# One kernel for sorted attention, a Fourier mix and an MLP: V of the first two batches mixed from its natural layout

## The chip, the cores and the metric

The kernel runs on one core of a Trainium2 chip. What counts is the device time of one execution, in microseconds (us). The engines named below are PE (TensorE: it loads a stationary operand and then streams a moving one past it), PEld (those loads of stationary operands, shown as a row of their own), DVE (VectorE), ACT (ScalarE), POOL (GpSimd, which here mainly starts transfers) and SP (SyncE, which starts the stores). "L945" is line 945 of the kernel; lines of the kernel before and of the changed kernel differ by up to some 16, and where both are meant the text says which.

## The reference

There are 4 batches, 8 heads, a sequence of 768 and 64 dimensions per head. `sort_net` holds an 8x8 matrix per batch and head. The rest in order, cut to what is computed:

```
P = sort_net
for _ in range(5):                       # on 8x8, per batch and head
    P = exp(P - max(P));  P = P / (rowsum + 1e-9);  P = P / (colsum + 1e-9)
k_sorted = einsum('bhij,bhjcd->bhicd', P, k in 8 blocks of 96 keys)
v_sorted = einsum('bhij,bhjcd->bhicd', P, v in 8 blocks of 96 keys)
attn     = softmax(0.125 * q_block @ k_sorted_block.T) @ v_sorted_block
x   = attn with heads side by side                     # 4 x 768 x 512
u   = x + real(fft(fft(x, axis=seq), axis=model))
un  = (u - mean(u)) / sqrt(var(u) + 1e-6)
out = u + maximum(un @ w_ch1, 0) @ w_ch2               # 512 -> 2048 -> 512
```

So 256 small matrices (4 batches x 8 heads x 8 blocks) mix the eight blocks of K and of V, attention runs inside a block of 96 keys, and the Fourier mix and the MLP then run over whole batches.

## The kernel before

**How the order of the work is set.** The program records every operation as an entry of a list, with a number. The table `ORDER` (written out as strings of numbers) gives for each of PE, DVE, ACT, POOL and SP the order in which that engine gets its entries. A scheduler then walks the tables and only picks PSUM banks and buffers. No engine leaves its order: an instruction whose input is late holds up everything behind it on its engine. Ahead of a point early in the program, PE waits are filled with dummy matmuls (L1973, "spins" below), which keep PE busy and have no reader.

**The start.** The 8x8 matrices are normalised on ACT and DVE (L766 to L776, tile `hr`), and spread into the block matrices `bdk` (for K, L805) and `bdv` (for V, L985) that serve as moving operands or stationary operands on PE.

**V of batches 0 and 1.** V is handled in two pairs of batches, t=0 (batches 0 and 1) and t=1 (batches 2 and 3). 128 partitions hold the (batch, head, block) triples of a pair; along a partition lie 96 keys of 64 dimensions. `v_path(t)` sums V over the keys (L873 on PE, L880 on DVE), which gives a mean that is handled apart. For t=0 the transfer puts V into the buffer `hr` (two transfers of 48 keys each), and eight copies (L903, issued through the helper at L855) rewrite it to `vcx` so that for one dimension d the 96 keys lie side by side; in that copy the keys of a block are also put in another order, (r, c) with r counting 6 and c counting 16. For t=1 a subtraction of the mean (L909) does the rewriting. `v_mix(t, e)` (L928) then does, for each of two halves e, 64 matmuls at L945: the stationary operand is 128 neighbouring columns of `vcx` starting at column 96d (96 columns for d=63), the moving operand 64 columns of `bdv`. Eight of them share a PSUM bank, and L951 adds the mean. The copy at L962 takes the bank to `vsf`/`vsb`, in front of the attention.

**K.** K is mixed by `bdk` on PE (L1140, L1170) and comes out of PSUM by a copy (L1148, L1178, again through L855; tile `ks`), with the keys in the same (r, c) order as V. Scores are L1236, the exponentials L1245, L1258 and L1260, the weighted sum of V L1275.

**The Fourier mix and the norm.** The work of a batch lies in two groups of three row tiles (T = 0 to 2 and T = 3 to 5). For a group of batch 0, the row sums of squares are taken on ACT (L1488), then one `Ln` (L1500) and one `Exp` (L1504) give the inverse of the deviation for the three row tiles, `nm` follows on DVE, `un` (L1518 on ACT, L1522 on DVE) is the normalised row, it is transposed, and the first MLP product L1558 reads it together with the weights `w1sb`. ACT evaluates `Exp` and `Ln` from tables which an instruction loads. At L711 the kernel asks for the set that has both functions, as the first thing on ACT.

**The MLP.** Batches 0 and 1 use plain products (L1558, L1615). Batches 2 and 3 use a scheme with seven products in place of eight (`ff1_seven`, L1694): some blocks of the hidden layer come out as a sum of a bank and a snapshot of another bank (`snap`, L1714 on ACT). DVE adds the two (L1702) and clamps the sum at zero (L1708). Second products are L1794, their sums L1811.

**The stores.** SP starts them in the order of its table. For T < 2 it is one transfer (L1583), or two halves (L1580); T = 2 takes three transfers (L1585, L1587, L1589); T > 2 goes through POOL (L1593).

Of the kernel before, what the change touches and what calls it, by code (L numbers as in the profile page):

```python
# [8 lines left out]

# [9 lines left out]
D = 64  # L19
NB = 8  # L20
# [46 lines left out]
    ),  # L67
    "ACT": (
# [24 lines left out]
    ),  # L93
    "DVE": (
# [1911 lines left out]
```

## Time and profile before

| what | value |
|---|---|
| median of 3 runs | 256.93 us (256.84 to 257.6) |
| span of the profiled execution | 254.8 us |
| PE busy | 245.2 us (96%), 2996 matmuls |
| DVE busy | 234.2 us (92%), 597 instructions |
| ACT busy | 165.3 us (65%), 376 instructions |
| POOL busy | 57.5 us (23%) |
| granted TensorE clock | full in all slices but the last |

Two things about reading it. The span runs from the first to the last recorded event of one profiled execution; the time that counts has about 2.1 us around it (256.93 - 254.8). And a matmul's record on PE is longer than the distance to the next one, since matmuls overlap: "busy" on PE means that something is in the pipe, not that PE could take nothing more. What PE needs per matmul is read from stretches in which many of the same kind follow each other, for instance in the chain of waits.

### The profile page before, as it was taken

To read this page: it belongs to the slowest core of one execution; us is meant where nothing else is said; L and a number is where in the kernel's file an instruction comes from. 1 tells how busy PE (TensorE), PEld (TensorE's weight loads), DVE (VectorE), ACT (ScalarE), POOL (GpSimd) and SP (SyncE) were. 2 spreads that over 40 slices of the span, in tenths; PEclk is the share of its full clock that TensorE was granted. 3 is DMA by queue.
4 is the path that set the end of the run, shared out by engine and by line. 5 is a ranking of instruction groups with operands and counts; after the bars stand their busy time and mean duration, and the time that the engine had idled before them with its cause. 6 is when DMAs were issued, how large, how long until landed. Compare 5 with 4: busy or idle time off the path is not lost.

```text
span 254.8 us, 7461 instructions
## 1 busy us (share of the span) xinstructions
PE 245.2 (96%) x2996; PEld 167.0 (66%) x2996; DVE 234.2 (92%) x597; ACT 165.3 (65%) x376; POOL 57.5 (23%) x88
## 2 busy tenths in 40 slices
PE   4999999999999999999999999999999999999992
PEld 1347875566566676644667757888657887567882
DVE  4799998999999989978999998999999999999993
ACT  2599998999968879956797377622687323773000
POOL 8974532234400770003100000210100000050013
PEclk9999999999999999999999999999999999999998
DMA  6999999999942699524132002530202400220025
GB/s 134 202 215 300 210 217 214 208 211 187 150 49 75 86 193 120 64 43 136 44 38 44 1 8 46 98 125 35 82 3 41 84 3 0 85 88 37 3 82 207
DMA packets 42809, 26.54 MB, mean 104 GB/s; under 512 B 30234, under 2 KB 39208, under 8 KB 42772
## 3 DMA queue, kind: packets, MB, share of 16 engines
q0 software_dynamic: 23664, 18.35, 42.9%
q1 hardware_dynamic: 19110, 7.71, 15.0%
q8 instruction: 23, 0.38, 0.6%
q14 instruction: 12, 0.10, 0.1%
HBM read 29.07 MB, written 6.29 MB: 139 GB/s over the span
## 4 chain that ended last, share of the span: by engine, by line
PE 71%; issue 9%; DVE 9%; ACT 8%; POOL 2%; DMA 1%; POOLq 0%; DVEq 0%
PE bank L1558 15%; PE bank L1794 14%; PE bank L1694 12%; PE bank L1615 9%; PE bank L1275 4%; PE bank L1440 3%; PE bank L945 2%; PE bank L1236 2%; ACT vcx L855 2%; PE bank L1349 2%; POOL out_dram L1593 2%; DVE rt L1292 1%; PE bank L1444 1%; PE bank L1047 1%; PE bank L1140 1%
## 5 line engine op out<-in xcount | busy, mean ns | idle before, releaser
L1558 PE MATMUL bank<-ut,w1sb 128*128 128x384 f16 x256 | 48.2, 326 | 0.0
L1714 ACT COPY vsf<-bank 128x384 f32<-128x384 f32 x48 | 21.6, 482 | 24.0 <-PE bank L1694 23.6
L1245 ACT ACTIVATE ex<-bank 96x384 f32<-96x384 f32 x64 | 29.3, 487 | 7.6 <-PE bank L1236 6.2
L1558 PEld LDWEIGHTS <-w1sb 128*128 128x128 f16 x256 | 23.1, 98 | 14.1 <-issue 0.3
L1570 ACT ACTIVATE hr<-bank 128x384 f16<-128x384 f32 x56 | 26.3, 491 | 8.5 <-PE bank L1558 8.5
L1593 POOL DMA_INDIRECT out_dram<-u,rows x9 | 9.4, 1042 | 97.4 <-DVE u L1811 72.5
L1794 PEld LDWEIGHTS <-hr 128*128 128x128 f16 x288 | 28.2, 98 | 4.6
L1702 DVE TENSOR_TENSOR hr<-bank,vsf 128x384 f16<-128x384 f32 x48 | 25.2, 548 | 1.6 <-PE bank L1694 1.0
L1615 PE MATMUL bank<-w2sb,hr 128*128 128x512 f16 x96 | 23.6, 380 | 0.0
L1794 PEld LDWEIGHTS <-vcx 128*128 128x128 f16 x216 | 21.1, 98 | 3.2
L1694 PE MATMUL bank<-ut,w1sb 128*128 128x384 f16 x96 | 20.7, 326 | 0.0
L1794 PE MATMUL bank<-w2sb,hr 128*128 128x256 f16 x144 | 18.7, 272 | 0.0
L1275 PEld LDWEIGHTS <-eb 97*128 97x128 f16 x416 | 15.7, 98 | 3.1 <-issue 0.4
L1794 PE MATMUL bank<-kq,vcx 128*128 128x256 f16 x144 | 17.5, 272 | 0.0
L1694 PEld LDWEIGHTS <-w1sb 128*128 128x128 f16 x128 | 12.5, 98 | 7.5
L612 POOL DMA_DIRECT2D kq<-in_q_dram x18 | 15.4, 866 | 8.8 <-PE bank L1558 4.2
L1292 DVE TENSOR_TENSOR rt<-bank,rz 128x384 f16<-128x384 f32 x32 | 16.9, 547 | 0.2
L1275 PE MATMUL bank<-vsf,eb 97*128 97x65 f16 x416 | 16.9, 193 | 0.0
L855 ACT CAST ks<-bank 128x384 f16<-128x384 f32 x27 | 14.4, 555 | 3.1 <-PE bank L1140 3.0
L1260 ACT ACTIVATE eb<-ex,negone 96x384 f16<-96x384 f32 x26 | 15.9, 616 | 0.1
L855 ACT CAST vsf<-bank 96x512 f16<-96x512 f32 x22 | 14.2, 679 | 1.4 <-PE bank L945 1.4
L1258 DVE TENSOR_SCALAR eb<-ex 96x384 f16<-96x384 f32 x38 | 13.9, 371 | 0.6 <-ACT ex L1245 0.4
(195 smaller groups left out, 535.5 us busy)
## 6 DMA issues: line engine op xcount, KB each, us to landing
w1sb<-in_moe_w_ch_dram POOLq DMA_DIRECT2D x4, 512.0 KB, 18.6
w2sb<-in_moe_w_ch_dram POOLq DMA_DIRECT2D x4, 512.0 KB, 21.5
hr<-in_v_dram POOLq DMA_DIRECT2D x2, 768.0 KB, 8.8
kq<-in_v_dram POOLq DMA_DIRECT2D x2, 768.0 KB, 12.7
kq<-in_k_dram POOLq DMA_DIRECT2D x8, 192.0 KB, 6.5
kq<-in_q_dram POOLq DMA_DIRECT2D x16, 96.0 KB, 6.7
out_dram<-u SPq DMA_DIRECT2D x5, 256.0 KB
kq<-in_k_dram POOLq DMA_DIRECT2D x2, 384.0 KB, 11.7
```

The costliest lines, as they stand in the source:

```text
L855: (nc.scalar.copy if e == "ACT" else V.tensor_copy)(dst, src)
L1245: nc.scalar.activation(ex.ap[0:96], pss[h2].ap[0:96, 0:384], AF.Exp, scale=SCALE),
L1260: nc.scalar.activation(ed, src, AF.Identity, bias=negone[0:96])
L1275: nc.tensor.matmul(po.ap[:, 65 * T:65 * T + 65], eb.ap[:, e0:e0 + 128], vsf[0:97, vi:vi + 65], start=(n == 0), stop=(n == len(WIN[T]) - 1) ...
L1292: P.add({"DVE": (0.465, 0.56)}, lambda _: V.tensor_tensor(rt.ap[:, :, D * h:D * h + D], po3()[:, :, 0:D], rz.ap[:, :, None].broadcast_to([ ...
L1558: nc.tensor.matmul(ps.ap[:, 0:GT], w1sb[:, c, 128 * fc:128 * fc + 128], ut.ap[:, c, :], start=(c == 0), stop=(c == 3))
L1570: nc.scalar.activation(hr[g][:, fc, :], ps.ap[:, 0:GT], AF.Relu)
L1615: nc.tensor.matmul(ps.ap, hr[g][:, fc, 128 * tt:128 * tt + 128], w2sb[:, fc, :], start=(fc == 0), stop=(fc == 15))
L1694: nc.tensor.matmul(ps.ap[:, 0:GT], lhs[:, c, fi], rhs()[:, c, :], start=(start and c == 0), stop=(c == 1), skip_group_check=True)
L1702: return P.add({"DVE": (0.47, 0.57)}, lambda _: V.tensor_tensor(hr[g][:, fc, :], p.ap[:, 0:GT], o.ap, op=ALU.add), r=r, w=hk(g, fc, fc + 1 ...
L1714: P.add({"ACT": act(GT)}, lambda _: nc.scalar.copy(x.ap, A.ap[:, 0:GT]), r=[A], w=[x], prio=pr_v - 1, tag="pc", after=avs)
L1794: nc.tensor.matmul(ps.ap[:, o:o + 256], lhs()[:, fc], rhs[:, fc], start=(start and fc == 0), stop=(fc == 7), skip_group_check=True)
```

## The change

There are four parts.

1. V of batches 0 and 1 is loaded straight into `vcx` in its natural layout (key, dimension). The eight copies are gone. The stationary operand of the matmuls for t=0 is now taken with a step: for dimension d it is 96 columns, each 64 elements (128 bytes) from the next. The matmul with the mean covers 96 columns too. Each group of eight matmuls now waits for the whole of `vcx`, as every group reads all keys.
2. Keys stay in natural order. The copy of `ks` out of PSUM writes other runs (of 3 or 6 elements) and reads PSUM with a step; the subtraction for t=1 reads and writes runs of 48 keys.
3. In `ff1_seven` one custom DVE instruction (`TENSOR_ADD_SAT`, which adds and holds the sum between 0 and the largest float) takes the place of add and clamp. 48 clamps are gone, 24 for each of the batches 2 and 3.
4. The entries have new numbers, so all tables of `ORDER` are written anew, and they don't give the same sequence.

The core of the diff, without the tables:

```diff
-    nat = [hr[0].rearrange("p a b -> p (a b)"),
+    nat = [vcx[:, 0:6144],
            kq[:, 4:8, :].rearrange("p a b -> p (a b)")]
...
-            if t == 0:
-                c = {"ACT": act(768, 0.75)}
-                if n not in (0, 2):
-                    c["DVE"] = dve(768)
-                P.add(c, lambda e, dst=dst, src=src: copy(e, dst, src),
-                      r=[("nat", 0, hf)] + half(hf),
-                      w=[("vcx", n)], tag="vcp",
...
-                    m = 96 if d == D - 1 else 128
+                    m = VM if t == 0 else 96 if d == D - 1 else 128
+                    lhs = (vcx[:, d:d + D * (m - 1) + 1:D] if t == 0 else
+                           vcx[:, 96 * d:96 * d + m])
                     nc.tensor.matmul(
-                        ps.ap[0:m, 64 * dd:64 * dd + 64],
-                        vcx[:, 96 * d:96 * d + m], bd,
+                        ps.ap[0:m, 64 * dd:64 * dd + 64], lhs, bd,
...
-                e, ks.ap.rearrange("p i (r c e) -> p e r i c", e=2, c=8)[
-                    :, half, 0:6],
-                pss[half].ap[:, 0:384].rearrange("p (r i c) -> p r i c", i=NB,
+                e, ks.ap[:, :, 0:BLK].rearrange(
+                    "p i (c e r) -> p e i c r", e=2, c=8)[:, half],
+                pss[half].ap[:, 0:384].rearrange("p (r i c) -> p i c r", i=NB,
                                                  c=8)),
...
-                return P.add({"DVE": (0.47, 0.57)}, lambda _: V.tensor_tensor(
-                    hr[g][:, fc, :], p.ap[:, 0:GT], o.ap,
-                    op=ALU.add), r=r, w=hk(g, fc, fc + 1), prio=pr_v,
-                    tag="fadd")
-
-            def relu(g, fc):
-                P.add({"DVE": (0.16, 0.24)}, lambda _: V.tensor_scalar(
-                    hr[g][:, fc, :], hr[g][:, fc, :], 0.0, None, op0=ALU.max),
+                return P.add({"DVE": (0.47, 0.57)}, lambda _: V._custom_dve(
+                    TENSOR_ADD_SAT, out=hr[g][:, fc, :], in0=p.ap[:, 0:GT],
+                    in1=o.ap, s0=FMAX, s1=0.0), r=r,
+                    w=hk(g, fc, fc + 1), prio=pr_v, tag="fadd")
...
     "ACT": (
-        "11 34 41 48 55 62 85 83 84 89 140 82 124 126 128 98 76 132 213 212 "
+        "34 41 48 55 62 116 82 132 90 118 207 136 120 98 140 138 124 104 122 "
```

The entry with number 11 is the request for the table set (L711 before, L712 now). It was first in ACT's table and now stands at place 190 of ACT's 354 rows. The rows below show three places of the sequence.

The first is the start of ACT, from the first instruction to the first copies of sorted keys (`hr_73` is the 8x8 matrices, `hr_72` the staged V, `ks` the sorted keys, `vb` the mean of V). Before:

```order
L711 ACT_TABLE_LOAD
L766 ACTIVATE hr_73<-hr_73 32x64 x5
L855 COPY vcx<-hr_72 128x96x8 x4
L855 CAST ks_77<-bank_64 128x3x8x16
L888 ACTIVATE vb<-vsum 128x128
L855 CAST ks_78<-bank_65 128x3x8x16
```

Now:

```order
L767 ACT_TABLE_LOAD
L767 ACTIVATE hr_73<-hr_73 32x64 x5
L856 CAST ks_77<-bank_64 128x8x16x3
L886 ACTIVATE vb<-vsum 128x128
L856 CAST ks_78<-bank_65 128x8x16x3
```

The four copies are gone from ACT here; the four of DVE are gone in the same way. The load of the table that stands first now belongs to the `Exp` at L767, not to the request.

The second place is the norm of the first group of batch 0 on ACT, just ahead of the first MLP product (`mv` holds sums, `ny` the inverse deviation, `nm` the shifted mean, `un` the normalised rows). Before:

```order
L1488 ACTIVATE ex_84,mv_129<-u_94,mv_129 128x512
L1488 ACTIVATE ex_83,mv_129<-u_95,mv_129 128x512
L855 CAST ks_77<-bank_62 128x6x8x8
L1500 ACTIVATE ny_131<-mv_129,eps 128x3
L1504 ACTIVATE ny_131<-ny_131 128x3
L1518 ACTIVATE un_100<-u_94,nm_133,ny_131 128x512
L855 COPY qt_81<-bank_63 128x384
```

Now:

```order
L1481 ACTIVATE ex_84,mv_129<-u_94,mv_129 128x512
L1481 ACTIVATE ex_82,mv_129<-u_95,mv_129 128x512
L856 CAST ks_78<-bank_65 128x8x8x6
L1493 ACT_TABLE_LOAD
L1493 ACTIVATE ny_131<-mv_129,eps 128x3
L1497 ACT_TABLE_LOAD
L1497 ACTIVATE ny_131<-ny_131 128x3
L1238 ACTIVATE ex_84<-bank_62 96x384
L1238 ACTIVATE ex_82<-bank_63 96x384
L1511 ACTIVATE un_100<-u_95,nm_133,ny_131 128x512
```

Two table loads stand between the sums and `ny`, and two more copies of scores between `ny` and `un`. ACT has 8 table loads in all where it had 1: the one at the start, these two, two around the norm of the second group of batch 0, and three around the norm of the first group of batch 1 and the request.

The third place is the end of SP, which starts the last stores. Before:

```order
L1585 DMA out_dram<-u_98 112x512
L1587 DMA out_dram<-u_98 15x512
L1589 DMA out_dram<-u_98 1x512
L1583 DMA out_dram<-eb_76 128x512
L1580 DMA out_dram<-u_97 128x256 x2
L1583 DMA out_dram<-u_93 128x512
```

Now:

```order
L1576 DMA out_dram<-eb_76 128x512
L1576 DMA out_dram<-u_95 128x512
L1573 DMA out_dram<-u_96 128x256
L1578 DMA out_dram<-u_98 112x512
L1580 DMA out_dram<-u_98 15x512
L1582 DMA out_dram<-u_98 1x512
```

The last store was one transfer and is now the one that takes three.

More of the change, by code (lines that the diff above doesn't have):

```diff
@@ L8 @@
 from concourse._compat import with_exitstack
+from concourse.dve_ops import TENSOR_ADD_SAT
 F32 = mybir.dt.float32
@@ L170 @@
 GT = 384
+VM = 96
+VW = 6144
+FMAX = float(np.finfo(np.float32).max)
 def _consts():
@@ L535 @@
     hr = [ct(f"hr{g}", [128, 16, GT], F16) for g in range(2)]
-    vcx = ct("vcx", [128, 128 * D + 2], F16)
-    dtab = vcx[:, 6144:7168].rearrange("p (c w) -> p c w", c=4)
-    lt = vcx[0:97, 7168:7168 + LTW]
+    vcx = ct("vcx", [128, VW + 2050], F16)
+    dtab = vcx[:, VW:VW + 1024].rearrange("p (c w) -> p c w", c=4)
+    lt = vcx[0:97, VW + 1024:VW + 1024 + LTW]
     vsf = ct("vsf", [128, 128 * (D + 1)], F16)
@@ L576 @@
     bdv32 = [ct("bdv32_0", [128, 16, NB], F32),
-             vcx[:, 7938:8194].bitcast(F32).rearrange(
+             vcx[:, VW + 1794:VW + 2050].bitcast(F32).rearrange(
                  "p (g i) -> p g i", i=NB)]
@@ L683, in load_v @@
             vv[128 * t:128 * t + 128, 48 * hf:48 * hf + 48, :], 1572864,
-            [("nat", t, hf)] + (hk(0, 8 * hf, 8 * hf + 8) if t == 0 else
-                                kqk(4 + 2 * hf) + kqk(5 + 2 * hf)), prio)
+            [("nat", t, hf)] + (
+                 [("vcx", n) for n in range(hf, 8, 2)] if t == 0 else
+                 kqk(4 + 2 * hf) + kqk(5 + 2 * hf)), prio)
     def load_w1(c, prio):
@@ L865, in v_path @@
         psm = Buf("pm", "pf") if t else Buf("pm")
-        stage = [i for n in range(4, 8) for i in kqk(n)] if t else hk(0)
-        def half(hf):
-            return stage if t else hk(0, 8 * hf, 8 * hf + 8)
+        stage = [i for n in range(4, 8) for i in kqk(n)] if t else []
         for hf, lo, hi in ((0, 0, 6), (1, 0, 3), (1, 3, 6)):
@@ L878, in v_path @@
             P.add(pe(mm(512, hi - lo) * (1.0 if t else 1.2), hi - lo), f,
-                  r=[("nat", t, hf), "pack"] + half(hf), w=[psm], tag="psm")
+                  r=[("nat", t, hf), "pack"] + stage, w=[psm], tag="psm")
         P.add({"DVE": (0.6, 0.68)}, lambda _: V.tensor_reduce(
@@ L891, in v_path @@
             r=["vsum"], w=["vb", "vb2"], tag="vb")
-        vcd = vcx[:, 0:6144].rearrange("p (d r c) -> p d r c", r=6, c=16)
+        if t == 0:
+            return
+        vcd = vcx[:, 0:6144].rearrange("p (d c) -> p d c", c=BLK)
         for n in range(8):
@@ L895, in v_path @@
             dr = slice(16 * qd, 16 * qd + 16)
-            src = n3[:, 48 * hf:48 * hf + 48, dr].rearrange(
-                "p (c r) d -> p d r c", r=6)
-            dst = vcd[:, dr, :, 8 * hf:8 * hf + 8]
-            if t == 0:
-                c = {"ACT": act(768, 0.75)}
-                if n not in (0, 2):
-                    c["DVE"] = dve(768)
-                P.add(c, lambda e, dst=dst, src=src: copy(e, dst, src),
-                      r=[("nat", 0, hf)] + half(hf),
-                      w=[("vcx", n)], tag="vcp",
-                      after=sks[30:31] if n in (0, 2) else sks[-1:])
-            else:
-                P.add({"DVE": dve(768, 1.0, 0.55)},
-                      lambda _, dst=dst, src=src, dr=dr: V.tensor_tensor(
-                          dst, src, vbn[:, dr, None, None].broadcast_to(
-                              [128, 16, 6, 8]), op=ALU.subtract),
-                      r=[("nat", 1, hf), "vbn"] + stage,
-                      w=[("vcx", n)], tag="vcd")
+            cr = slice(48 * hf, 48 * hf + 48)
+            P.add({"DVE": dve(768, 1.0, 0.55)},
+                  lambda _, cr=cr, dr=dr: V.tensor_tensor(
+                      vcd[:, dr, cr], n3[:, cr, dr].rearrange(
+                          "p c d -> p d c"), vbn[:, dr, None].broadcast_to(
+                          [128, 16, 48]), op=ALU.subtract),
+                  r=[("nat", 1, hf), "vbn"] + stage,
+                  w=[("vcx", n)], tag="vcd")
     def v_mean():
@@ L951, in f @@
                     nc.tensor.matmul(
-                        ps.ap, sel[:, n:n + 1].broadcast_to([128, 128]),
+                        ps.ap[0:VM], sel[:, n:n + 1].broadcast_to([128, VM]),
                         xm.ap, start=False, stop=True, skip_group_check=True)
             mixed = P.add(pe(*((0.47, 9) if t == 0 else (0.26, 8))), f,
-                  r=[("vcx", i) for i in range(2 * (n // 2), min(
-                      8, 2 * ((8 * n + 8) // 16) + 2))] + [("bdv16", t)]
+                  r=[("vcx", i) for i in (range(8) if t == 0 else range(
+                      2 * (n // 2), min(8, 2 * ((8 * n + 8) // 16) + 2)))]
+                  + [("bdv16", t)]
                   + ([xm, "pack"] if t == 0 else []),
@@ L1178, in kqt @@
                 P.add(evac(384), lambda e, half=half, ps=ps: copy(
-                    e, ks.ap.rearrange("p i (r c) -> p r i c", c=16)[
-                        :, 3 * half:3 * half + 3],
-                    ps.ap[:, 0:384].rearrange("p (r i c) -> p r i c", i=NB,
+                    e, ks.ap[:, :, 0:BLK].rearrange(
+                        "p i (c r) -> p i c r", c=16)[
+                        :, :, :, 3 * half:3 * half + 3],
+                    ps.ap[:, 0:384].rearrange("p (r i c) -> p i c r", i=NB,
                                               c=16)),
@@ L1722, in pair @@
             add(0, i, D, x, [D, x])
-            relu(0, i)
             prod(Q, G1, e_(E1), ["g1", E1], True)
@@ L1729, in pair @@
             add(1, i + 8, Q, x, [Q, x])
-            relu(1, i + 8)
             prod(A, X22, e_(E4), w1k + [E4], False)
@@ L1736, in pair @@
             add(1, i, Q, x2, [Q, x2])
-            relu(1, i)
         for i in range(8):
```

2 lines of the change are left out of this document (removed), and 198 rows, old and new, of the table ORDER.

## The prediction

> **What bounds the kernel now.** I read the busy time of the engines first by stages of the span, then the chain of waits in order of time, then the groups of instructions. In the rows by stages the columns are the busy time on PE, PEld, DVE, ACT and POOL with the number of instructions, then the clock, the DMA share and GB/s.
>
> ```profile
> 0.00:20.00 20.00, 15.51 (x115) 7.07 (x116) 14.83 (x51) 12.30 (x23) 16.16 (x26) 1.00 1.03 193
> 20.00:51.00 31.00, 30.54 (x605) 21.21 (x606) 29.39 (x82) 28.96 (x68) 11.05 (x17) 1.00 1.13 225
> 51.00:60.00 9.00, 8.92 (x175) 5.92 (x172) 8.08 (x27) 8.57 (x25) 3.00 (x4) 1.00 1.25 209
> 60.00:150.00 90.00, 89.97 (x1329) 56.84 (x1328) 84.73 (x189) 68.70 (x160) 17.02 (x25) 1.00 0.67 82
> 150.00:250.30 100.30, 100.26 (x782) 76.01 (x780) 96.71 (x252) 46.77 (x106) 9.72 (x17) 1.00 0.20 56
> ```
>
> PE reads full everywhere, but its records overlap, so this does not say who sets the pace. The chain (start, length, what) does:
>
> ```profile
> 10.12 5.66 ACT vcx L855 x4
> 19.40 0.34 PE bank L945 x8
> 25.70 0.34 PE bank L945 x8
> 30.84 0.47 DVE rt L1292
> 41.41 0.70 DVE bdk L832
> 45.55 1.50 ACT ex L1488 x4
> 47.05 0.47 ACT ks L855
> 53.52 0.48 ACT hr L1570
> 59.24 1.09 PE bank L1037 x8
> 78.35 0.93 PE bank L945 x32
> 184.98 10.40 PE bank L1694 x64
> ```
>
> From 28 to 42 us its pieces are nearly all of DVE, from 45 to 59 of ACT and DVE, and from 59 on of PE in long runs. So there are three regimes. Up to about 59 us, DVE (29.39 of 31 us) and ACT (28.96 of 31, then 8.57 of 9) set the pace. After that it is PE, and work taken from DVE there is taken from beside the path. ACT has 21 us to spare in 60 to 150.
>
> **The copies of V.** They are these two groups (busy us, mean ns), with what stands around them in the timeline of ACT and DVE:
>
> ```profile
> L855 ACT COPY vcx<-hr 128x768 f16<-128x768 f16 x4 | 5.8, 1509 | 0.0
> L855 DVE COPY vcx<-hr 128x768 f16<-128x768 f16 x4 | 3.2, 808 | 0.0
> 15.69 0.46 ACT L855 CAST ks<-bank 128x384 f16<-128x384 f32 x1
> 11.53 0.80 DVE L855 COPY vcx<-hr 128x768 f16<-128x768 f16 x1
> 13.56 1.29 DVE L805 TENSOR_TENSOR bdk<-bank,pack 128x512 f16<-128x512 f32 x2 [0.17 <-PE bank L799]
> 16.37 0.81 DVE L855 COPY vcx<-hr 128x768 f16<-128x768 f16 x1
> ```
>
> The 5.66 us of ACT on the chain are not a gain of 5.66: the next thing ACT does is the first `ks`, and that reads a product with `bdk`, which DVE ends at 13.56 + 1.29 = 14.85. Two of the DVE copies stand just before `bdk`, partly in the gaps of its exchange with PE; I put 1.0 us of their 1.6 on the path. The other two (the second at 17.52, as long) have work close behind them: 2 x 0.81 = 1.6. That makes 2.6 us, taken as the gain of this part. Bounds: 1.6 (the late pair alone) and 5.66 (the whole chain piece). The value is near the lower one because `bdk` holds ACT.
>
> The gain can't bring the first MLP product forward. Its first start, and issue and landing of its weights:
>
> ```profile
> L1558 PE MATMUL bank<-ut,w1sb x256: 323/326/337, 51.0 to 155.2; 128*128 128x384 f16 x128
> L612 POOL DMA_DIRECT2D w1sb<-in_moe_w_ch_dram x4: 531/537/548, 27.3 to 30.8; - x4
> DMA to landing us min/median/max: 16.2/18.6/20.1
> ```
>
> The last weights are issued at 30.8 and, at the longest of these landings, there at 50.9; the product starts at 51.0. POOL's loads keep their sequence, so a shorter head shows only as other PE work done before 51. The new sequence of PE does have more there: 39 more weighted sums (L1275), 32 more scores (L1236) and 24 more key products (L1140). At the price of the chain's small matmuls (0.93 us for 32, so 29 ns) they are at most 95 x 29 = 2.8 us, about what the copies free. I book the 2.6 once and nothing for the sequence.
>
> **The table loads.** The row of the one load, and the norm of the first group as ACT runs it now:
>
> ```profile
> L711 ACT ACT_TABLE_LOAD x1 | 1.3, 1283 | 0.7 <-PEq L1990 0.7
> 47.38 0.29 ACT L1500 ACTIVATE ny<-mv,eps 128x3 f32<-128x3 f32 x1
> 47.71 0.20 ACT L1504 ACTIVATE ny<-ny 128x3 f32<-128x3 f32 x1
> 48.14 0.81 ACT L1518 ACTIVATE un<-u,nm,ny 128x512 f16<-128x512 f32 x1 [0.23 <-DVE nm L1506]
> ```
>
> Seven loads are new, at 1283 ns each: 9.0 us of ACT. They fall in three places.
>
> The first two stand just ahead of `ny`: 2.57 us. Behind them wait `nm` and all three `un`, and on ACT the score copies and `qt`, which feed PE. ACT is on the chain here, so I take the full +2.57 (bounds 0.5, if they use up the 2.04 us that ACT idles in 20 to 51, and 2.57).
>
> The next two belong to the second group, in 51 to 60, where ACT has 0.43 us free. But PE then has the first group's products, which don't need that norm. I take half, +1.28 (bounds 0 and 2.57).
>
> The last three lie later, where ACT has 21 us free: 0 (bound 3.85, if that cover is gone and the norm of batch 1 is what PE waits for).
>
> [...]
>
> **The strided weight loads.** The trace has loads of three widths:
>
> ```profile
> L945 PEld LDWEIGHTS <-vcx 128*128 128x128 f16 x252 | 10.0, 98 | 3.2 <-issue 0.2
> L945 PEld LDWEIGHTS <-vcx 128*96 128x96 f16 x4 | 0.5, 124 | 0.0
> L1349 PEld LDWEIGHTS <-eo 128*1 128x1 f16 x8 | 0.3, 80 | 1.0 <-issue 0.6 <-DVE eo L1325 0.3
> ```
>
> A load of one column takes 80 ns, one of 128 takes 98, one of 96 takes 124. So 96 columns are dearer than 128: 44 ns above the load of one column against 18. A matmul of L945 comes every 29 ns; if the load sets the pace at 96 columns it is 44, so 15 ns more. All 128 such matmuls of t=0: 1.9 us. On the chain before 51 us are five groups of eight (the first and last are shown), 40 x 15 = 0.6; the rest lies where DVE and ACT set the pace. I take +0.6. Bounds: 0, and a price per line that has no row on PE (a rival below). The wait for the whole of `vcx` costs nothing by these rows: the last copy runs at 17.52 and reads the second half of V, so both had landed before the first L945 at 19.40.
>
> [...]
>
> **The clamp.** What goes is the second row; the first becomes the fused instruction:
>
> ```profile
> L1702 DVE TENSOR_TENSOR hr<-bank,vsf 128x384 f16<-128x384 f32 x48 | 25.2, 548 | 1.6 <-PE bank L1694 1.0 <-ACT vsf L1714 0.3
> L1708 DVE TENSOR_SCALAR hr<-hr 128x384 f16<-128x384 f16 x48 | 10.3, 250 | 0.1
> ```
>
> DVE loses 10.3 us, all after 164, where PE has 100.26 busy of 100.30 in runs like the 64 products of L1694 in 10.40 us (162 ns each). PE hides it: 0. A custom instruction has no row. If it takes 548 + 250 = 798 ns, DVE is as before; beyond that it has 3.6 us of slack (100.30 - 96.71), then it is on the path. Bounds: 0, and for one twice as long as the add, 48 x (1096 - 798) - 3.6 = +10.7.
>
> The new runs in the copies of `ks` and in L909 I put at 0: the elements are as many, and both layouts have short runs. One way of erring is 27 x 0.555 = 15 us of ACT work (0.555 is the mean of `ks` there) growing by a tenth, 1.5, most of it beside DVE or PE.
>
> **The tail.** Stores as SP starts them, and DVE's last instruction:
>
> ```profile
> 250.30 0.42 DVE L1811 TENSOR_TENSOR u<-bank,u 128x256 f32<-128x256 f32 x1 [0.34 <-PE bank L1794]
> 244.28 0.32 SPq L1585 DMA_DIRECT2D out_dram<-u  x1
> 244.65 0.43 SPq L1587 DMA_DIRECT2D out_dram<-u  x1
> 245.12 0.25 SPq L1589 DMA_DIRECT2D out_dram<-u  x1
> 250.75 0.33 SPq L1583 DMA_DIRECT2D out_dram<-u  x1
> ```
>
> The last store takes three issues in place of one: 0.32 + 0.43 + 0.25 - 0.33 = +0.67 (bounds 0, if the large first part lands last, and 0.76, with the gaps: 245.12 + 0.25 - 244.28 - 0.33).
>
> **The sum.** -2.6 + 2.57 + 1.28 + 0.6 + 0 + 0.67 = +2.5. On the span: 254.8 + 2.5 = 257.3; with the 2.1 us that the median has around it, 259.5. Its own range is 257.5 (no cost of the second pair and of the tail: -1.95) to 262 (second pair in full, all strided loads on the path: +2.6).
>
> **The rivals.**
>
> Faster: the loads find cover. ACT's idle time (2.04 us in 20 to 51) and the 1.2 us that `ks` can come earlier (15.69 against a `bdk` that ends 1.0 to 1.6 sooner) hold the first pair, PE has more work in front of the first product, and the strided loads hide behind DVE. Then -2.6 is all: 254.3. For it: 51.0 is set by the weights as much as by the norm. Against it: the loads stand at the latest point before the product.
>
> No change: the freed head pays for the loads and the rest is hidden, 256.9. This needs both sides to be within 0.8 us of each other.
>
> Far slower: each column of a strided load touches another place in memory and costs as such a read costs ACT. ACT copied 768 elements with a step in 1509 ns; without one it takes:
>
> ```profile
> L855 ACT COPY qt<-bank 128x768 f16<-128x768 f16 x3 | 2.4, 793 | 0.0
> ```
>
> Doubling 44 gives 88 ns; adding 716 / 768 = 0.93 ns for each of 96 columns gives 133. Against 29, the 40 matmuls on the chain cost 2.4 or 4.2 us, and half of the other 88, 2.6 or 4.6: together 5.0 or 8.8 in place of 0.6, so 263.9 or 267.7. It decides as soon as a load takes more than some 60 ns. Against it: PE may read one column from all partitions at a time, so a step need not matter.
> [...]
>
> Slower by the fused instruction, as worked out above: 270.
>
> **How the numbers follow.** Likeliest, +2.5: 0.40. Faster with cover: 0.28. No change: 0.13. A price per line: 0.15. A slow fused instruction: 0.04. A measurement tells 0.3% (0.8 us) from no change. Faster is then 0.28, same 0.13, slower 0.40 + 0.15 + 0.04 = 0.59. The range: 253.8 leaves out the lower third of the faster case (0.08), 266.0 the upper half of the price per line (0.07) and the slow fused instruction (0.04), in all 0.19.
>
> **What would show it.** Eight table loads on ACT, four of them between about 47 and 62 us, with `un` later by some 2.5 us and the first product at 53 to 54: right on the main term; if it starts at 51 to 52, the faster case. Loads of 96 columns at 124 ns and groups of eight at some 0.45 us: right on the stride; at 170 ns or more, the price per line. The fused instruction at 550 ns and DVE less busy after 164 with PE as full as now: right on the clamp. Last store three issues after DVE's last instruction: the tail. I am wrong if PE's runs after 60 us have changed in length, since I changed nothing there, or if the later three loads show up as PE waiting.

## The result and the profile after

The changed kernel takes 289.41 us (median of 6 runs, 285.15 to 290.35) against 256.83 us before. Three of the six (289.57 to 290.35) count as slow; the fast ones have a median of 288.92 us, from which the differences below are taken, and a ratio of 1.120 to the kernel before (95% interval 1.113 to 1.128). The forecast was 259.5 us, in a range up to 266.0. The direction was right, the size was wrong by an order of magnitude: +32.1 us where +2.5 stood. (The expectations of t11 and b_strided were written with 289.41.)

The profile is of the run of 285.15 us, the shortest of the six. The first rows to read are the stages again, with the columns as in the prediction (us on PE, PEld, DVE, ACT, POOL, then clock, DMA share, GB/s).

```profile
20.00:51.00 31.00, 30.79 (x395) 26.65 (x394) 18.75 (x52) 17.65 (x38) 11.11 (x17) 0.83 1.14 226
51.00:60.00 9.00, 9.00 (x80) 6.49 (x81) 3.75 (x11) 2.82 (x7) 3.10 (x4) 0.63 1.25 206
150.00:200.00 50.00, 49.99 (x526) 36.13 (x524) 48.23 (x118) 32.10 (x76) 1.74 (x3) 1.00 0.20 45
```

In 20 to 51 us PE runs 395 matmuls where it ran 605, while ACT and DVE, which set the pace there before (28.96 and 29.39 us), now have 17.65 and 18.75. The roles have changed: they wait for PE (between 20 and 60 us the copies to `vsf` on ACT wait 8.7 us and those on DVE 6.6 us for the matmul with the mean, L942). And the granted clock, 1.00 before, is 0.83 and then 0.63. Those are means: in the same trace the clock is 0.50 for two stretches of some 10 us, which begin at 26 and at 53 us, and 1.00 around them. After 150 us the stage looks as it did. The chain of waits (start, length, what) names what PE does in that stage:

```profile
18.02 1.42 PE bank L937 x8
19.67 1.17 PE bank L937 x8
...
56.60 1.45 PE bank L937 x8
...
68.57 1.28 ACT L1493
...
77.23 1.28 ACT L1493
...
79.22 1.28 ACT L1238
```

All sixteen groups of eight strided matmuls (two halves of eight groups) are pieces of it, at 1.17 to 1.45 us each; before, eight groups of t=0 stood there, five at 0.34 us and three at 0.23 to 0.25. Behind them come table loads on ACT; besides the three shown, those at 70.18, 130.91 and 132.90 us are on the chain too. The groups of weight loads, of table loads, of the fused instruction, and the first MLP product:

```profile
L937 PEld LDWEIGHTS <-vcx 128*96 128x96 f16 x130 | 22.7, 253 | 1.5 <-issue 1.1
L937 PEld LDWEIGHTS <-vcx 128*128 128x128 f16 x126 | 5.3, 98 | 1.9
L1493 ACT ACT_TABLE_LOAD x3 | 3.8, 1283 | 0.1
L1497 ACT ACT_TABLE_LOAD x2 | 2.6, 1283 | 0.0
L1695 DVE CUSTOM_DVE_ANT_0 hr<-bank,vsf 128x384 f16<-128x384 f32 x48 | 24.8, 550 | 4.8 <-PE bank L1687 3.3 <-ACT vsf L1702 1.2
L1551 PE MATMUL bank<-ut,w1sb x256: 323/326/337, 75.5 to 180.5; 128*128 128x384 f16 x128
```

A strided load of 96 columns shows 253 ns, twice the 124 of the four 96-column loads before. From one matmul's start to the next it is 163 ns (median of the 112 neighbouring pairs of t=0), where 44 was forecast and 29 was there. It is 163 at a clock of 1.00 (70 pairs) and at 0.50 (41 pairs) alike. The fused instruction takes 550 ns, the add alone took 548. The first MLP product starts at 75.5 us, 24.5 later than before.

### The profile page after: what moved, and what is told of

Its sections match the earlier page's. It is cut to its first block, busy times and chain, and to the rows that moved or that the text cites. A ratio compares the mean times of both kernels' runs of the same rounds, so it can differ in the third digit from the quotient of the medians.

```text
span 283.3 us, 7376 instructions
## 1 busy us (share of the span) xinstructions
PE 265.9 (94%) x2988; PEld 186.5 (66%) x2988; DVE 229.2 (81%) x562; ACT 161.8 (57%) x362; POOL 57.2 (20%) x88
## 4 chain that ended last, share of the span: by engine, by line
PE 80%; ACT 7%; DVE 6%; DMA 3%; issue 2%; POOL 1%; POOLq 0%; DVEq 0%; ACTq 0%
PE bank L1551 14%; PE bank L1779 13%; PE bank L1687 13%; PE bank L937 9%; PE bank L1608 7%; PE bank L1268 4%; PE bank L1342 3%; PE bank L1229 3%; DMA vcx<-in_v_dram 3%; PE bank L1433 2%; PE bank L942 2%; DVE u L1796 2%; DVE vcx L1755 2%; ACT L1493 1%; PE bank L871 1%
## 5 line engine op out<-in xcount | busy, mean ns | idle before, releaser
L937 PEld LDWEIGHTS <-vcx 128*96 128x96 f16 (+1 forms) x256 | 27.8, 177 | 3.3 <-issue 1.1
L937 PE MATMUL bank<-bdv,vcx 128*96 128x64 f16 (+1 forms) x256 | 29.3, 263 | 0.0
L1695 DVE CUSTOM_DVE_ANT_0 hr<-bank,vsf 128x384 f16<-128x384 f32 x48 | 24.8, 550 | 4.8 <-PE bank L1687 3.3
L1586 POOL DMA_INDIRECT out_dram<-u,rows x9 | 10.0, 1114 | 89.5 <-DVE u L1796 58.1
L856 ACT CAST vsf<-bank 96x512 f16<-96x512 f32 x23 | 15.3, 674 | 11.0 <-PE bank L942 8.7
L1779 PE MATMUL bank<-kq,vcx 128*128 128x256 f16 x144 | 18.2, 273 | 0.0
L856 ACT CAST ks<-bank 128x384 f16<-128x384 f32 x22 | 10.8, 512 | 11.8 <-PE bank L1162 9.2
L1285 DVE TENSOR_TENSOR rt<-bank,rz 128x384 f16<-128x384 f32 x32 | 17.1, 548 | 0.2
## 6 DMA issues: line engine op xcount, KB each, us to landing
w1sb<-in_moe_w_ch_dram POOLq DMA_DIRECT2D x4, 512.0 KB, 18.3
out_dram<-u SPq DMA_DIRECT2D x5, 256.0 KB, 2.2
```

Of the source, the lines that this page charges most:

```text
L856: (nc.scalar.copy if e == "ACT" else V.tensor_copy)(dst, src)
L937: nc.tensor.matmul(ps.ap[0:m, 64 * dd:64 * dd + 64], lhs, bd, start=(t == 1 or dd == 0), stop=(t == 1), skip_group_check=(t == 0))
L1285: P.add({"DVE": (0.465, 0.56)}, lambda _: V.tensor_tensor(rt.ap[:, :, D * h:D * h + D], po3()[:, :, 0:D], rz.ap[:, :, None].broadcast_to([ ...
L1695: return P.add({"DVE": (0.47, 0.57)}, lambda _: V._custom_dve(TENSOR_ADD_SAT, out=hr[g][:, fc, :], in0=p.ap[:, 0:GT], in1=o.ap, s0=FMAX, s ...
L1779: nc.tensor.matmul(ps.ap[:, o:o + 256], lhs()[:, fc], rhs[:, fc], start=(start and fc == 0), stop=(fc == 7), skip_group_check=True)
```

## The experiments

The blocks of code below are cut to the lines that matter. In c128, s128, mix_steps, b_strided and b_wide the matmul with the mean also gets the new number of columns. The kernels with another stationary operand mix wrong elements, as their expectations say.

### Is it the loads, and is it their step or their count?

Three kernels keep the change and its sequence and alter only the stationary operand of t=0; a fourth gives each of the eight groups another form.

```diff
 # c128                                            (changed kernel)
-                    m = VM if t == 0 else 96 if d == D - 1 else 128
+                    m = 96 if d == D - 1 else 128
-                    lhs = (vcx[:, d:d + D * (m - 1) + 1:D] if t == 0 else
-                           vcx[:, 96 * d:96 * d + m])
+                    lhs = vcx[:, 96 * d:96 * d + m]
 # c96: the lhs of c128, with m as in the change
 # s128
+                    m = 128 if t == 0 else 96 if d == D - 1 else 128
+                    d_ = d % 48
+                    lhs = (vcx[:, d_:d_ + 48 * 127 + 1:48] if t == 0 else
 # mix_steps: group n has FORMS[n] = (columns, step)
+FORMS = [(102, 1), (97, 2), (98, 4), (99, 8), (100, 16), (101, 32),
+         (96, 64), (128, 48)]
```

> The changed kernel with one thing undone: the stationary operand of t=0 is again 128 neighbouring columns (96d to 96d+127 of vcx). V lies there in its natural layout, so the matmuls mix the wrong elements; their number and size are those of the kernel before. In the changed kernel the loads of L937 with 96 columns take 253 ns where the neighbouring 128 took 98, groups of eight take 1.42 us on the chain where they took 0.34, and the first MLP product starts at 74.9 us where it started at 51.0. If the weight loads are the whole of the loss (theory A), loads go back to 98 ns, the clock to 1.00 up to 60 us, and the time is what the other terms of my sum give: 256.93 - 2.6 + 2.57 + 1.28 + 0.67 = 258.9 (257 to 261). If the new sequence and the table loads make a good part of it (theory B), the time stays above 265.

> The changed kernel with 96 neighbouring columns (96d to 96d+95) as stationary operand of t=0: the count of the change without its step. The matmuls mix the wrong elements. If the step costs (each column of a strided load touching another place), loads take the 124 ns of the four 96-column loads of before, the matmuls follow each other every 44 ns, and the time is within 2 us of that with 128 neighbouring columns. If the count costs (a load is only fast with 128 columns), loads stay near 250 ns and the time stays above 280.

> The changed kernel with 128 columns as stationary operand of t=0, each 48 elements (96 bytes) from the next: a step without the count. It starts at d modulo 48, so that it stays inside V, and mixes the wrong elements; the matmul with the mean covers 128 columns. If the step costs, a load has 128 columns at the price of now 96, so 160 / 96 x 128 = 213 ns at full clock, and the time is 289 or more. If the count costs, loads take 98 ns as neighbouring ones do, and the time is that with 128 neighbouring columns, near 259.

> The changed kernel with another form of stationary operand in each of the eight groups of t=0, told apart by their column counts: 102 columns with step 1, 97 with step 2, 98 with 4, 99 with 8, 100 with 16, 101 with 32, 96 with 64, 128 with 48. Wrong elements are mixed. If the step costs by places touched, 102 at step 1 is near 44 ns from matmul to matmul, prices rise up to some step and stay there, and 128 at step 48 is the dearest. If the count costs, all forms but 128 take about one ns and a half per column, and 128 at step 48 takes 29 ns.

Measured, each against 257.27 us for the kernel before: c128 265.38 us (ratio 1.035, 1.029 to 1.040), c96 266.49 (1.036, 1.032 to 1.041), s128 268.43 (1.045, 1.042 to 1.049), mix_steps 278.77 in one run. The loads, from the groups of the three kernels in that order:

```profile
L936 PEld LDWEIGHTS <-vcx 128*128 128x128 f16 x252 | 10.2, 98 | 3.3 <-issue 0.3
```

```profile
L936 PEld LDWEIGHTS <-vcx 128*96 128x96 f16 x130 | 7.5, 124 | 1.2 <-issue 0.3
```

```profile
L938 PEld LDWEIGHTS <-vcx 128*128 128x128 f16 x254 | 15.0, 133 | 3.0 <-issue 0.3
```

(The last row averages 128 strided loads and 126 neighbouring ones at 98.) And of mix_steps:

```profile
L940 PEld LDWEIGHTS <-vcx 128*97 128x97 f16 x16 | 0.9, 125 | 0.1
L940 PEld LDWEIGHTS <-vcx 128*98 128x98 f16 x16 | 1.7, 185 | 0.1
L940 PEld LDWEIGHTS <-vcx 128*99 128x99 f16 x16 | 3.1, 276 | 0.2 <-issue 0.2
L940 PEld LDWEIGHTS <-vcx 128*101 128x101 f16 x16 | 2.9, 263 | 0.2 <-issue 0.2
```

From the start of one matmul to the next, medians worked out from the traces of c128, c96, mix_steps and s128:

```
columns  step (elements, bytes)   ns from matmul to matmul
128       1     2                  29     (c128)
 96       1     2                  45     (c96)
102       1     2                  48     (7 pairs at full clock; 87 for the 7 at half clock)
 97       2     4                  46
 98       4     8                  93
 99       8    16                 182
100      16    32                 187
101      32    64                 172
 96      64   128                 163
128      48    96                  65     (s128, and the same in mix_steps)
```

Where not said otherwise, the pairs are at full clock, or the median is the same at both (step 8: 182 and 182).

Neither theory alone holds. The count alone costs 16 ns a matmul and, with 128 of them, no difference in time that these intervals can tell (1.1 us between the medians of c96 and c128). The step alone costs 36 ns a matmul and 3.1 us. Both together cost 134 ns a matmul and 288.92 - 265.38 = 23.5 us. In the rows of 96 to 102 columns the price grows with the step, from 46 ns at 2 elements to 93 at 4 and 182 at 8 elements (16 bytes), and from there to 64 elements it is 163 to 187, about 1.7 to 1.9 ns a column.

c128 also leaves 265.38 - 257.27 = 8.1 us to explain that have nothing to do with the stride.

### The table loads, and the step by itself

```diff
 # c128_t11 (on c128) and t11 (on the changed kernel): entry 11 to the front of ACT's table
-        "34 41 48 55 62 116 82 132 90 118 207 136 120 98 140 138 124 104 122 "
+        "11 34 41 48 55 62 116 82 132 90 118 207 136 120 98 140 138 124 104 "
 # b_late (on the kernel before): entry 11 from the front to place 205 of ACT's table
 # b_strided (on the kernel before)
-                    m = 96 if d == D - 1 else 128
+                    m = 96 if t == 0 or d == D - 1 else 128
-                        vcx[:, 96 * d:96 * d + m], bd,
+                        vcx[:, d:d + 64 * (m - 1) + 1:64] if t == 0 else
+                        vcx[:, 96 * d:96 * d + m], bd,
```

> The changed kernel with neighbouring 128 columns (265.38 us) and, beside that, the request for the table set first on ACT again, as in the kernel before. The chain of the kernel without that shows table loads of 1.28 us as its own pieces at 47.45, 58.09, 109.79 and 111.77, and DVE's last instruction ends 6.7 us before the end of the span, where it was 4.1. If the table loads make the 8.5 us that are left beside the strided loads (theory A): four to five loads on the path, 5 to 7 us back, 258.5 to 260.5, with 2 to 3 us left for the tail. If the new sequence of the engines makes it (theory B): less than 2 us back, 263.5 or more.

> The changed kernel with nothing but the request for the table set moved back to the front of ACT. One table load is left in place of eight. Loads stand on its chain at 68.57, 77.23 and 79.22 us. Theory A: they cost here as they do with neighbouring columns, 4 to 7 us less, 282.5 to 285.5. Theory B, or the strided loads hiding the table loads: within 2 us of 289.4.

> The kernel before with nothing but the request for the table set moved to a place behind the norm of the first group of batch 1, as in the change: eight table loads in place of one. Theory A: 5 to 7 us slower, 262 to 264; by my own sum 2.57 + 1.28, so 260.8. Theory B: within 1.5 us of 256.9.

> The kernel before with nothing but the form of the stationary operand of t=0 changed: 96 columns, 64 elements apart, out of vcx; the copies stay, and the matmuls mix the wrong elements. The run of mixed forms gave 163 ns from matmul to matmul for 96 columns at step 64 at full clock, against 29 for 128 neighbouring ones: 128 x 134 = 17.2 us, of which the waits of PE before 51 us hide a part. If the price of the loads is all, 266 to 274. If the clock that goes down with them (0.83 and 0.63 in 20 to 60 us of the changed kernel) adds to it, as 289.41 - 265.38 = 24.0 us between the changed kernel with and without the step says, 276 to 281 and a clock under 0.9 in the stage.

Measured, each against 257.18 us for the kernel before: c128_t11 258.46 us (ratio 1.005, 1.003 to 1.007), t11 281.21 (1.093, 1.087 to 1.100), b_late 268.31 (1.045, 1.042 to 1.047), b_strided 278.71 (1.085, 1.082 to 1.089).

The seven table loads cost 265.38 - 258.46 = 6.9 us in the changed sequence without the step, 7.7 us with it (288.92 - 281.21), and 11.1 us in the sequence of before. That is above every expectation for b_late. Its ACT in the timeline (start, length, what):

```profile
47.55 1.28 ACT L1500 ACT_TABLE_LOAD   x1
48.84 0.30 ACT L1500 ACTIVATE ny<-mv,eps 128x3 f32<-128x3 f32 x1
49.16 1.28 ACT L1504 ACT_TABLE_LOAD   x1
50.45 0.20 ACT L1504 ACTIVATE ny<-ny 128x3 f32<-128x3 f32 x1
50.88 0.81 ACT L1518 ACTIVATE un<-u,nm,ny 128x512 f16<-128x512 f32 x1 [0.23 <-DVE nm L1506]
```

`un` starts at 50.88 in place of 48.14. A load starts 0.02 us behind the instruction before it, and the next starts 0.01 us after its end, so a load costs its 1283 ns, and nothing more is seen around it. In the chain of the same kernel the other five are pieces too:

```profile
61.56 1.28 ACT L1500
...
63.64 1.28 ACT L1504
...
116.32 1.28 ACT L1500
117.93 1.28 ACT L1504
...
123.31 1.28 ACT L711
```

All seven are on the path: 7 x 1.28 = 9.0 us. "ACT has 21 us free between 60 and 150" was true and no cover. A load stands in ACT's fixed sequence, and what PE waits for next stands behind it: on the chain the load at 123.31 us is followed by the exponentials of L1245 at 124.60, and the next matmuls (L1140) start at 125.14. What is left of the 11.1, some 2 us, comes together with a granted clock of 0.83 between 50 and 70 us of that kernel, where the kernel before has 1.00; no run separates the two.

b_strided is the step without anything else of the change: +21.5 us, against 17.2 from the price of the loads.

### Where the rest of the step's price comes from

```diff
 # b_wide (on b_strided, t = 0 only)
+                        nc.tensor.matmul(
+                            ps.ap[0:m, 256 * (dd // 4):256 * (dd // 4) + 256]
+                            .rearrange("p (a w) -> p a w", w=64),
+                            vcx[:, d:d + 64 * (m - 1) + 1:64],
+                            bd[:, None, :].broadcast_to([128, 4, 64]),
```

> The kernel before with the 96 strided columns as stationary operand (as measured at 278.71 us) and with a moving operand four times as wide: the 64 columns are streamed four times in each of the 128 matmuls, into half a bank in place of 64 columns of it, so the mix is wrong in size and place. 256 columns took 109 ns in L1440, which fits beside a load of 163. If the low clock comes from the array streaming too little beside each load, and costs time, the clock goes up towards 1.00 in 30 to 70 us and the time falls, by up to 278.71 - 256.9 - 17.2 = 4.6 us, to 274 to 277, although PE streams 128 x 192 columns more. If the clock does not follow the streamed columns, or costs nothing, the time stays at 278.7 or rises.

Measured: 274.62 us against 257.52 (ratio 1.067, 1.065 to 1.069). It streams four times the columns and is 4.1 us faster than b_strided. The stages of b_strided and then of b_wide:

```profile
30.00:40.00 10.00, 10.00 (x101) 8.66 (x102) 4.25 (x11) 4.25 (x10) 2.98 (x5) 0.66 1.08 216
40.00:50.00 10.00, 9.98 (x143) 8.72 (x139) 6.69 (x23) 6.53 (x15) 2.81 (x4) 0.93 1.11 213
50.00:60.00 10.00, 10.00 (x73) 7.75 (x74) 3.36 (x7) 3.06 (x7) 3.09 (x4) 0.50 1.25 205
60.00:70.00 10.00, 10.00 (x145) 5.47 (x148) 8.53 (x25) 8.76 (x22) 3.91 (x5) 0.89 1.65 132
```

```profile
30.00:40.00 10.00, 9.90 (x138) 8.75 (x137) 5.70 (x18) 5.50 (x13) 3.20 (x5) 1.00 1.08 216
50.00:60.00 10.00, 9.86 (x127) 7.67 (x126) 4.83 (x12) 5.43 (x13) 3.09 (x4) 1.00 1.25 206
60.00:70.00 10.00, 10.00 (x186) 5.85 (x188) 8.86 (x28) 9.63 (x24) 3.91 (x5) 1.00 1.87 144
```

The clock goes from 0.50 to 0.93 up to 1.00. The loads are as dear as before (166 ns from matmul to matmul), and 274.62 - 257.52 = 17.1 us is left, which is the 17.2 of 128 x 134 ns. So the loss of the step has two parts: about 17 us of slow loads, of which nothing is hidden, and about 4 us that go with the clock, which was 0.50 to 0.93 with 64 columns streamed per 163 ns and 1.00 with 256. The strided loads themselves did not get dearer by it, as their 163 ns at both clocks show. Other matmuls did: in the profile of the changed kernel the distance from a matmul with the mean to the group behind it is 232 ns at full clock and 433 at half, and in mix_steps 102 neighbouring columns went from 48 to 87. PE's busy row says 9.9 to 10.0 of 10 in both kernels and shows none of this.

### The parts that were to help, and the end

```diff
 # b_nocopy (on the kernel before)
-    nat = [hr[0].rearrange("p a b -> p (a b)"),
+    nat = [vcx[:, 0:6144],
-                P.add(c, lambda e, dst=dst, src=src: copy(e, dst, src),
+                P.add(c, lambda e: None,
 # b_fused (on the kernel before): the fused instruction of the change in `add`; in `relu`
-                P.add({"DVE": (0.16, 0.24)}, lambda _: V.tensor_scalar(
-                    hr[g][:, fc, :], hr[g][:, fc, :], 0.0, None, op0=ALU.max),
+                P.add({"DVE": (0.16, 0.24)}, lambda _: None,
 # b_tail3 (on the kernel before)
+            elif T == 0 and b == 3:
+                st_ = [nc.sync.dma_start(out[b, t0 + lo:t0 + hi, :], u.ap[lo:hi])
+                       for lo, hi in ((0, 112), (112, 127), (127, 128))]
 # b_half (on the kernel before)
+            elif T == 0 and b == 3:
+                st_ = [nc.sync.dma_start(out[b, t0:t0 + 128, m], u.ap[:, m])
+                       for m in (slice(0, 256), slice(256, 512))]
 # c128_t11_one (on c128_t11)
+            elif T == 2 and b == 3:
+                st_ = [nc.sync.dma_start(out[b, t0:t0 + 112, :],
+                                         u.ap[0:112])]
```

> The kernel before with V of batches 0 and 1 loaded straight into vcx and the eight copies left out, everything else in its place; the stationary operand stays 128 neighbouring columns, so the matmuls mix the wrong elements. My term for the copies was -2.6 us (bounds 1.6 and 5.66): 254.3 if it was right. Rival: the first MLP product is held at 51 us by its weights (landed at 50.9) and the sequence of PE is that of before, so there is no other work to bring forward and it is within 0.8 us of 256.9.

> The kernel before with the fused instruction in ff1_seven and the 48 clamps left out, nothing else. The fused instruction measured 550 ns in the changed kernel against 548 for the add. My term: 0, as PE sets the pace after 164 us, so 256.9 within 0.5. Rival: DVE, at 96.7 of 100.3 us busy, held PE now and then, and it gives 1 to 3 us.

> The kernel before with its last store cut into the three transfers of the change's last store (112, 15 and 1 rows), nothing else. By my term +0.67, so 257.6. By the tails of the two profiles (6.7 us behind DVE's last instruction with the change's sequence, 4.1 before) +2.6, so 259.5.

> The kernel before with its last store cut into two column halves; the left half is ready about 0.7 us before the right one, so only 128 KB instead of 256 KB leave behind DVE's last instruction. If what lies behind the last store grows with its bytes, 0.5 to 1 us less, 256.0 to 256.4, which would beat both kernels. If it is a fixed time, within 0.3 us of 256.9.

> The changed kernel with neighbouring columns and the table request first (258.46 us), and its very last store as one transfer of 112 rows; the last 16 of its 128 rows are left out. Its last DVE instruction ends at 249.4 us and its span at 256.0, 6.6 us later, against 4.1 in the kernel before. If the two small transfers make that tail, about 2 us less, 256 to 257. If something else in the new sequence does, within 0.5 us of 258.5.

Measured: b_nocopy 1.0001 of the kernel before (0.9988 to 1.0013), b_fused 1.0000 (0.9991 to 1.0009), b_tail3 1.0004 (0.9991 to 1.0017), b_half 1.0005 (0.9994 to 1.0015). None of the four moves the time by what can be measured. The last, c128_t11_one, takes 258.44 us (1.0042, 1.0021 to 1.0063), as c128_t11 did with all three transfers.

Why the copies were worth nothing shows in ACT's timeline of b_nocopy, in the two instructions around the place where its four copies were:

```profile
9.88 0.26 ACT L766 ACTIVATE hr<-hr 32x64 f32<-32x64 f32 x1 [1.51 <-DVE hr L776]
15.35 0.48 ACT L855 CAST ks<-bank 128x384 f16<-128x384 f32 x1 [5.21 <-PE bank L1170]
```

The 5.8 us of copies have become 5.21 us of waiting for PE's product with `bdk`; `ks` starts 0.34 us earlier. On the chain of that kernel `bdk` starts where it did, and by 18.3 us both kernels are at the same matmul at the same time (the last line is of the kernel before, whose `bdk` is shown ahead of the forecast):

```profile
13.58 1.29 DVE bdk L805 x2
...
18.30 0.49 PE bank L999 x2
```

```profile
18.29 0.49 PE bank L999 x2
```

So all eight copies lay in gaps. For the clamp, the group and the stage of b_fused:

```profile
L1703 DVE CUSTOM_DVE_ANT_0 hr<-bank,vsf 128x384 f16<-128x384 f32 x48 | 24.7, 552 | 6.6 <-PE bank L1695 5.1 <-ACT vsf L1714 1.2
150.00:250.30 100.30, 100.30 (x783) 76.00 (x780) 89.63 (x204) 46.73 (x106) 9.71 (x16) 1.00 0.19 55
```

DVE has 89.63 us in place of 96.71, but the fused instruction waits 5.1 us for PE where the add waited 1.0. PE is as full as before (100.30 us, before 100.26), and the time is the same.

The end of c128_t11 is another matter. DVE's last instruction there ends at 249.4 us, 1.3 us before that of the kernel before, and yet its span is 1.2 us longer, 256.0. The stages at the end (the last but one number is the DMA share), of c128_t11 and then of the kernel before:

```profile
246.00:248.00 2.00, 2.00 (x21) 1.79 (x19) 1.97 (x6) 0.00 (x0) 1.70 (x3) 1.00 0.01 3
248.00:250.00 2.00, 0.96 (x9) 0.61 (x7) 1.25 (x3) 0.00 (x0) 1.81 (x3) 1.00 0.99 362
250.00:252.00 2.00, 0.00 (x0) 0.00 (x0) 0.00 (x0) 0.00 (x0) 0.59 (x1) 1.00 0.95 308
252.00:254.00 2.00, 0.00 (x0) 0.00 (x0) 0.00 (x0) 0.00 (x0) 0.00 (x0) 1.00 0.67 245
```

```profile
246.00:248.00 2.00, 2.00 (x21) 1.80 (x19) 2.00 (x6) 0.00 (x0) 0.69 (x1) 1.00 0.36 136
248.00:250.00 2.00, 2.00 (x21) 1.78 (x19) 1.96 (x6) 0.00 (x0) 1.61 (x5) 1.00 0.54 194
250.00:252.00 2.00, 0.26 (x3) 0.00 (x0) 0.42 (x1) 0.00 (x0) 0.81 (x1) 1.00 0.84 312
252.00:254.00 2.00, 0.00 (x0) 0.00 (x0) 0.00 (x0) 0.00 (x0) 0.00 (x0) 0.81 0.41 154
```

In the new sequence the last stores leave nearly together: hardly any traffic up to 248, then 4 us at 0.99 and 0.95. In the old one they begin earlier. That the bunching makes the longer end is read from these rows; no run moved the stores apart. That the three transfers don't make it is shown twice. The single runs of c128_t11_one lie between 257.3 and 259.6 us, so the 1.3 us of this sequence is a difference of medians that single runs need not show.

## Why the prediction was right or wrong

The 32.1 us divide, by differences of medians, into 23.5 for the strided operand (288.92 - 265.38), 6.9 for the table loads (265.38 - 258.46) and 1.3 for everything else (258.46 - 257.18); the small rest is the kernel before, which differs by 0.4 between the sets of runs.

**What bounds the kernel** was read correctly for the kernel before: after 60 us PE, as b_fused confirms. But "up to about 59 us DVE and ACT set the pace" was used as if it gave PE slack without limit. With 17 us more of loads PE is the bound of that stage, and nothing of them was hidden (b_wide: 17.1 us of 17.2).

**The copies, -2.6**: wrong, 0. Both halves of the term failed. The 1.0 for the early pair: without it `bdk` starts at 13.58 us as before, since DVE waits 1.16 us for PE's L799 there. The 1.6 for the late pair, "work close behind them: 2 x 0.81": without it DVE waits 0.87 us for PE and 0.39 for ACT, and from 19.55 us on it is where it was. That `bdk` holds ACT, the argument against 5.66, was right and should have been carried through to DVE.

**The table loads, +2.57, +1.28 and 0**: the seven loads at 1283 ns and the first pair were right (`un` starts 2.74 us later in b_late), the cover was not. Half for the second pair and nothing for the last three came from a mean of free time over a stage; in b_late all seven are pieces of the chain. Where the prediction had 3.85, the runs show 6.9, 7.7 and 11.1.

**The strided loads, +0.6**: the step of the prediction that failed most, with 23.5 us measured in the changed sequence and 21.5 alone. The rows had no strided load; I took the price of 96 neighbouring columns, 44 ns, which c96 confirms at 45, and then the share of the chain of before. Price (163) and share (all of it) were both wrong. The chain of before was also read too short: it has eight groups there, three of them under 0.34 us, which would have made the term 1.0. The rival that priced a place in memory per column came nearest, with 133 ns at its upper end, but it too let half of the loads off the chain hide, gave 267.7 at most, and got 0.15. That each column costs as a place in memory was its estimate and is not shown: 128 columns at a step of 96 bytes cost 65 ns. The lower clock, some 4 us, was in none of the cases.

**The clamp, 0**: right, and for the reason given. **The fused instruction** is as fast as the add (550 and 552 ns against 548). **The order, 0, and the tail, +0.67**: by b_tail3 three transfers cost 0 within 0.4 us. What the new sequence does at the end reads in the rows as stores that start close together, which no run tested; together with a work stream that ends 1.3 us earlier, +1.3.

By its own signs the prediction fell at once: loads at 253 ns where 170 or more stood for the price per line, the first product at 75.5 us where 53 to 54 stood, and two of the later three table loads on the chain.

What stays open: the step costs 23.5 us in the changed kernel and 21.5 in the one before. The loads and the clock explain the latter. For the 2 us between them the runs point at the clock. The profiled run of the changed kernel has a mean clock of 0.955 over its span and is 285.15 - 263.78 = 21.4 us above the profiled run of c128; the five longer ones have 0.922 to 0.937. The four runs of t11 go from 279.45 us at 0.951 to 283.16 at 0.931 in the same order. No run sets the clock alone in that sequence. The groups of eight differ in their first gap: it is 28 to 72 ns in the five of 1.17 us, all of which come straight behind a matmul with the mean, and 155 to 186 in the others; no run tested why.

No version here beats the kernel before. The best that the runs point to, a natural layout read 128 columns wide with the table request in front, would be an estimated 258.46 + 3.1 = 261.5 by their differences, since the copies that it saves cost nothing. No run shows it: s128 had a step of 48 elements and not 64, and it mixes wrong elements.

## What to carry to other kernels

Before a layout copy is removed, see whether anything waits for it, and what reads the data afterwards: the eight copies here lay in gaps, and the strided operand that took their place cost 17 us of loads and 4 more that went with the clock. A price from a neighbouring row holds for that row's form alone (45 ns for 96 neighbouring columns, 163 at the step); where two things change at once (count and step), look for what they do together, and ask what becomes the bound if the price is four times as high. And free time of an engine, as a sum over a stage, is no cover by itself: ACT had 21 us of it between 60 and 150 us, and the five table loads that b_late has there, which stood in ACT's fixed sequence ahead of what other engines waited for, were all on the chain. Put such an instruction on the chain first, and then look for a reason to take it off.

## What the runs showed of the hardware

- The price of a matmul with its load went by columns and step together: 29 ns from matmul to matmul for 128 neighbouring columns (c128), 45 for 96 (c96), 65 for 128 at a step of 96 bytes (s128), 163 for 96 at 128 bytes (the changed kernel). In the groups of 96 to 102 columns it grew with the step up to 16 bytes (46 ns at 4 bytes, 93 at 8, 182 at 16) and was 163 to 187 from there to 128 bytes.
- With 64 columns streamed per load of 163 ns (b_strided) the granted clock was 0.50 to 0.93 between 30 and 70 us (means of 10 us; in the trace of the changed kernel it is 0.50 or 1.00 at any time); with 256 columns per load (b_wide) it was 1.00, and that kernel was 4.1 us faster.
- With the request for the table set late, ACT loaded tables seven more times, at 1.283 us each with 0.01 to 0.02 us around them; in b_late all seven were on the chain. The time with the late request was 6.9 us (c128), 7.7 us (the changed kernel) and 11.1 us (b_late) longer than with the early one.
